# Rows of the small expert blocks scattered from a tile of their own, and weights loaded in other pieces, in an attention kernel with a routed expert layer

## The chip, the cores and the metric

One core of one Trainium2 chip runs the kernel. The metric is the device time of one execution in microseconds (us), the median over several runs. TensorE (PE in the rows, its weight loads PEld) multiplies matrices, VectorE (DVE), ScalarE (ACT) and GpSimd (POOL) work on elements, and SyncE (SP) issues most transfers (DMAs). A name with a q (ACTq, SPq) is an engine's own issuing part: it takes the instructions in order, and waits there for what an instruction needs.

## The reference, cut to what matters

```
scores = scale * (q @ k^T) - log(S);  x = sigmoid(scores) @ v     # 8 x 12 heads x 448 x 64
x = rows of 768 values, 3584 tokens
out = x                                                            # for tokens with x @ w_skip <= 0
e = argmax(x @ w_gate);  g = softmax(x @ w_gate)[e]                # 8 experts
out = x + g * (relu(x @ w1[e]) @ w2[e])                            # w1: 768 x 1024, w2: 1024 x 768
```

## The kernel before, in words

**Attention and routing.** The first 320 us or so are the attention, written out for 48 pairs of heads. Each batch's rows go to `out` as they are finished, the tokens are sorted by expert into a list in DRAM, and a small table is worked out on the chip: which blocks of tokens run, of which expert and of which kind. The first two blocks of the largest expert are written out by hand, beside the end of the attention.

**The loop over blocks.** The rest is a loop over the blocks of that table (L1535 to L1539). Each engine reads the kind of its block from the table and branches to one of four arms. A full block (`block(i, False)`) computes 128 tokens in split precision: every weight is held as a high part and a rest (`wh1`, `wl1`, `wh2`, `wl2`), and TensorE multiplies three times. A split block (`block(i, True)`) does the same, and beside it turns the raw weights of the next expert into those four sets: ScalarE writes the high parts (`hi1`, `hi2`), VectorE the rests (`lo1`, `lo2`). A half block (`half`, up to 64 tokens) and a few block (`few`, up to 32) multiply the raw weights once, in plain float32, and then load the raw weights of the next expert into the same tiles, by SyncE's queue. The order of the instructions on each engine is that of the program text; nothing is reordered by the framework.

The blocks of this input follow each other like this: split, half, full, half, full, few, full, few, full, few, split, few, full, few. The loop ends with a few block.

**What a block does with rows.** Rows come and go by indirect DMAs of GpSimd. In the block before its use, TensorE transposes the rows `xn` (`turn_x`, L489); as soon as that is done, `fetch` lets GpSimd gather the rows of the block after next into `xn` (L1269 to L1273, the gather is L561). So a gather has about one block of time. `fetch` also reads `rn` (L1270), the record that holds the rows' numbers, and ScalarE's queue loads the next record into `rn` in `next_rec` (L1105), which has to wait until L1270 has read the old one. At its end each block calls `put`: GpSimd writes the row numbers into `rp` (L1283, L1284), reads two of the results with a small add (`seen`, L1289) so that the scatter needs no wait of its own, and scatters the rows with an add into `out` (L571). L1283 overwrites what the last scatter read, so it waits until that scatter has landed.

**The rows of the results.** In a full block VectorE writes the results to `yt` and GpSimd copies them to `ys`, from which the scatter takes them. In half and split blocks VectorE writes `ys` itself. In few blocks ScalarE (L1441) and VectorE (L1443) write `yt`, and GpSimd copies it to `ys` in two halves (L1298), with a `seen` before each and one behind.

**The split block's order on ScalarE.** `whole_x`, `next_rec`, `hi2(0)`, `hi2(1)`, `hi_x`, `hi2(2)` to `hi2(5)`. On VectorE behind it: `lo2(0)` to `lo2(2)`, two casts (L1370), `lo_x` (L499), the weighted sum into `ys` (L1321), then `put` for GpSimd and `lo2(3)` to `lo2(7)`. `lo_x` reads the PSUM tile that the next block's `turn_x` writes, and the weighted sum reads the PSUM tile that the next block's second product writes.

**Raw weights.** `raw1` is held in three tiles and three loads (first half of the columns: rows 0 to 2 and 3 to 5 of the six 128-row pieces; second half: all six), `raw2` in four tiles of two pieces. Before the loop the last of the `raw2` loads goes through ScalarE's queue, the others through SyncE's.

Of the kernel before, what the change touches and what calls it, by code (L numbers as in the profile page):

```python
# [10 lines left out]
F32 = mybir.dt.float32  # L11
# [3 lines left out]
AF = mybir.ActivationFunctionType  # L15
ALU = mybir.AluOpType
# [3 lines left out]
P = 128  # L20
# [3 lines left out]
def kernel(  # L24
# [33 lines left out]
    SM = 32  # L58
# [1082 lines left out]

    parts1 = ((0, 0, 3), (0, 3, NK1), (1, 0, NK1))
    raw1g = []
    raw2g = []

    def some1(n):
        for _ in range(n):
            h, a, z = parts1[len(raw1g)]  # L1150
            raw1g.append(mo.tile([P, z - a, H1], F32, name=f"raw1_{h}_{a}"))

    def some2(n):
        for _ in range(n):
            raw2g.append(mo.tile([P, 2, DM], F32, name=f"raw2_{len(raw2g)}"))

    skips = []

    def skip(n):
        mo.tile([P, n], F32, name=f"skip_{len(skips)}")  # L1160
        skips.append(n)
# [12 lines left out]
    sv = mo.tile([P, 2, 2], F32, name="sv")  # L1174
    jk = mo.tile([P, 2], F32, name="jk")
    yt = mo.tile([P, DM], F32, name="yt")
    skip(4688 - DM)
    some1(1)
    some2(2)
    skip(128)  # L1180
    some2(2)
    raw1 = [[raw1g[i // 3][:, i % 3, :], raw1g[2][:, i, :]] for i in range(NK1)]
    raw2 = [raw2g[j // 2][:, j % 2, :] for j in range(NK2)]

    ph = [new_t(f"ph{h}") for h in range(2)]
    py = [new_t("py0"), ps_b.tile([P, 512], F32, tag="b", name="py1")]
# [3 lines left out]
    def next_expert(col):  # L1190
        return entry(NXT, col, SP, NE - 1), entry(HAS, col, SP, 1)

    def load_w1(n, nx):
        h, a, z = parts1[n]
        return nc.sync.dma_start(
            raw1g[n],
            w1[ds(nx[0], 1), a * P : z * P, h * H1 : (h + 1) * H1].rearrange(
                "o (i p) f -> p (o i) f", p=P
            ),
            cond=nx[1],  # L1200
        )

    def load_w2(g, nx, queue=nc.sync):
        queue.dma_start(
            raw2g[g],
            w2[ds(nx[0], 1), g * 2 * P : (g + 1) * 2 * P, :].rearrange(
                "o (i p) f -> p (o i) f", p=P
            ),
            cond=nx[1],
        )  # L1210
# [38 lines left out]
        nc.values_load(first_i[0:1, 0:1], engines=[ET.Activation], min_val=0, max_val=1),  # L1249
    )  # L1250

    for n in range(3):
        load = load_w1(n, nx)
        if n == 1:
            tc.add_manual_dep(
                load.ins,
                done.ins.name,
                mybir.DependencyInfo(mybir.DependencyClass.Sync, mybir.DependencyReason.DATA),
                reason="rows and code first",
            )  # L1260
        if n == 0:
            look_ahead(slice(2, 3))
    for g in range(4):
        load_w2(g, nx if g < 3 else nx_act, nc.sync if g < 3 else nc.scalar)

    def fetch():

# [10 lines left out]
    def next_rec(i):  # L1278
        load_rec(rn, ds(i + 5, 1), [ET.Activation], nc.scalar)

    def put(n, last=None):

        pool.tensor_tensor(rp[0], rid[:, 0:1], zero, op=ALU.add)  # L1283
        pool.tensor_tensor(rs, rp[0], zero, op=ALU.add)  # L1284
        if last is False:
            pool.drain()

        def seen(y, at):
            pool.tensor_tensor(  # L1289
                jk[:n], y[:n, at - 1 : at + 1], y[:n, at - 1 : at + 1], op=ALU.add  # L1290
            )

        if n == SM:

            for o in range(2):
                seen(yt, (o + 1) * H2 - 1)
                s = slice(o * H2, (o + 1) * H2)
                pool.tensor_copy(ys[:n, s], yt[:n, s])  # L1298
        if last is False:
            seen(yt, H2)  # L1300
            pool.tensor_copy(ys, yt)
        seen(ys, H2)
        out_rows = scatter(rp[0][:n], ys[:n], ALU.add)
        tc.declare_no_dep(out_rows.ins, group="got", across_iterations=True, reason="a token is in one block only")
        tc.add_to_no_dep_group("put", out_rows.ins)

    def advance(pieces=2):

# [73 lines left out]
    def few(i):  # L1382

        nx = named()
        take_rec()

        def quarter(dst, g, n, a, w, j, most):
            nc.tensor.matmul(  # L1388
                dst[g * SM : (g + 1) * SM, :n],
                a,  # L1390
                w,
                start=(j == 0),
                stop=(j == most - 1),
                tile_position=(0, g * SM),
            )

        turned = (pht[0], ph[0])
        parts = [slice(c * P, (c + 1) * P) for c in range(2)]
        for c, s in enumerate(parts):
            for j in range(NK1):  # L1400
                for g in range(4):
                    quarter(
                        ph[c], g, P, xf[:, j, :SM], raw1[j][c][:, g * P : (g + 1) * P], j, NK1
                    )
            nc.scalar.activation(hs[:, s], ph[c][:, :P], AF.Relu)
        for n in range(3):
            load_w1(n, nx)
        nc.tensor.transpose(turned[0][:, :P], hs[:, parts[0]], ident)
        for h in range(2):
            turn_x(xn, h, pxt[h])  # L1410
        fetch()
        nc.tensor.transpose(turned[1][:, :P], hs[:, parts[1]], ident)
        ht4 = ht[:, : 8 * SM].rearrange("p (c g t) -> p c g t", c=2, g=4)
        for s, p in zip(parts, turned):
            nc.scalar.activation(ht[:, s], p[:, :P], AF.Copy)
        ready_x()

        for n in range(4):
            c, j = n // 2, n % 2
            for g in range(4):  # L1420
                o, h = g // 2, g % 2
                m = 4 * c + 2 * h + j
                quarter(
                    py[h],
                    g,
                    H2,
                    ht4[:, c, 2 * h + j, :],
                    raw2[m][:, o * H2 : (o + 1) * H2],
                    n,
                    NK2 // 2,  # L1430
                )
        for g in range(4):
            load_w2(g, nx)
        look_ahead(ds(i + 3, 1))
        for m in range(2):
            for o in range(2):
                g = 2 * o + m
                s = slice(o * H2, (o + 1) * H2)
                p = py[m][g * SM : (g + 1) * SM, :H2]
                if not m:  # L1440
                    nc.scalar.activation(yt[:SM, s], p, AF.Copy, scale=recs[:SM, 0, 0:1])  # L1441
                    continue
                nc.vector.scalar_tensor_tensor(  # L1443
                    yt[:SM, s], p, recs[:SM, 0, 0:1], yt[:SM, s], op0=ALU.mult, op1=ALU.add
                )
        next_rec(i)
        put(SM)
        advance()

    def half(i):  # L1450

        nx = named()
        take_rec()

        def side(dst, g, n, a, w, j, most):
            nc.tensor.matmul(  # L1456
                dst[g * MD : (g + 1) * MD, :n],
                a,
                w,
                start=(j == 0),  # L1460
                stop=(j == most - 1),
                tile_position=(0, g * MD),
            )

        for j in range(NK1):
            for h in range(2):
                side(ph[0], h, H1, xf[:, j, :], raw1[j][h], j, NK1)
        turned = (pht[0], ph[1])
        parts = [slice(0, 2 * P), slice(2 * P, 4 * P)]
        for s in (slice(0, P), slice(P, 2 * P), parts[1]):  # L1470
            nc.scalar.activation(hs[:, s], ph[0][:, s], AF.Relu)
        for n in range(3):
            load_w1(n, nx)
# [27 lines left out]
        for g in range(4):  # L1501
# [66 lines left out]
```

## Time and profile before

| | us |
|---|---|
| median of 3 runs | 522.71 |
| lowest and highest run | 522.39, 524.77 |
| the profiled execution's own time | 522.76 |
| its span, first to last instruction | 520.4 |
| time of that execution outside its span | 2.36 |

The span is what the rows of the profile add up to; an edit that shortens the span by some amount shortens the time by the same, as the 2.36 us around it are not the kernel's instructions. In rows of the timeline the first number is the start in the span, the second the time from the first start to the last end of the instructions that are merged in that row, and the bracket tells how long the engine was idle before it and what ended that.

### The profile page before, as it was taken

How to read it: one execution, taken by the hardware profiler on the slowest of the kernel's cores; microseconds unless marked ns; L12 is line 12 of the kernel's file. 1: busy time of each engine (PE TensorE's matmuls, PEld its weight loads, DVE VectorE, ACT ScalarE, POOL GpSimd, SP SyncE). 2: the span in 40 equal slices, each digit the busy share in tenths (PEclk: the TensorE clock that was granted, in tenths of full speed). 3: DMA queues.
4: the chain of work that ended last, by engine and by line, in shares of the span. 5: the costliest groups of instructions: out<-in, count | busy, mean ns of one | idle time of the engine just before them, and what ended most of it. 6: DMA issues, size and time to landing. Idle time of an engine off the chain costs nothing.

```text
span 520.4 us, 15378 instructions
## 1 busy us (share of the span) xinstructions
PE 505.8 (97%) x5031; PEld 337.7 (65%) x5032; DVE 293.0 (56%) x692; ACT 278.3 (53%) x481; POOL 238.7 (46%) x355
## 2 busy tenths in 40 slices
PE   8999999999999999999999999999999999999991
PEld 6655545545545555555455889967769797979790
DVE  4556856658668688686694862682222322349522
ACT  5776776767767767667666212751122323258322
POOL 4523553443556675765674402232321434344534
PEclk9999999999999999999999999999999999999997
DMA  8999877997999999999965105949295879696943
GB/s 207 219 245 191 174 172 160 173 176 174 204 186 235 227 203 212 197 205 217 191 148 117 20 31 172 388 126 384 87 350 202 267 285 300 254 331 233 356 175 47
DMA packets 142082, 107.22 MB, mean 206 GB/s; under 512 B 99164, under 2 KB 114524, under 8 KB 142033
## 3 DMA queue, kind: packets, MB, share of 16 engines
q1 hardware_dynamic: 134048, 96.90, 71.3%
q0 software_dynamic: 4032, 8.51, 6.8%
q10 hardware_dynamic: 3952, 1.16, 1.1%
q8 instruction: 30, 0.49, 0.4%
q14 instruction: 20, 0.16, 0.1%
HBM read 98.49 MB, written 17.56 MB: 223 GB/s over the span
## 4 chain that ended last, share of the span: by engine, by line
PE 92%; DVE 2%; DMA 2%; issue 1%; ACT 1%; POOL 0%; ACTq 0%; POOLq 0%; DVEq 0%
PE s L209 25%; PE pa L237 23%; PE ph L513 11%; PE py L541 10%; PE b_ph L513 3%; PE b_py L541 3%; PE ph L1388 3%; PE py L1388 2%; PE ph L1456 2%; PE py L1456 2%; PE pxt L489 2%; PE pl L277 2%; PE pht L527 1%; DMA rn<-lst 1%; PE pg L294 1%
## 5 line engine op out<-in xcount | busy, mean ns | idle before, releaser
L229 ACT ACTIVATE at<-s,bias 128x896 f32<-128x896 f32 (+1 forms) x191 | 173.5, 914 | 81.2 <-PE s L209 73.2
L209 PE MATMUL s<-x 64*64 64x448 f32 (+1 forms) x1528 | 166.0, 497 | 1.7 <-DVE x L191 0.8
L237 PE MATMUL pa<-at,v 64*64 64x448 f32 (+1 forms) x1536 | 164.1, 489 | 0.0
L173 POOL COPY kq<-kq 32x896 f32<-32x896 f32 (+1 forms) x96 | 88.1, 917 | 95.9 <-DMA kq<-in_q_dram 49.6
L209 PEld LDWEIGHTS s<-x 64*64 64x64 f32 x1528 | 79.5, 191 | 54.2 <-issue 29.6
L237 PEld LDWEIGHTS pa<-at,v 64*64 64x64 f32 x1536 | 62.0, 133 | 56.4 <-issue 49.5
L191 DVE STREAM_TRANSPOSE x<-kq 128x448 f32<-128x448 f32 x94 | 80.7, 934 | 4.4 <-POOL kq L173 4.4
L247 DVE TENSOR_TENSOR xt<-xt,pa 128x448 f32<-128x448 f32 x48 | 29.8, 620 | 52.5 <-ACT xt L668 50.3
L411 POOL DMA_INDIRECT lst<-rec,idx x32 | 31.6, 987 | 16.1 <-issue 5.2
L483 POOL TENSOR_TENSOR wl<-wr,wh 128x384 fp32r<-128x384 f32 (+1 forms) x28 | 31.2, 1123 | 12.1 <-DVE wh L482 8.2
L252 DVE STREAM_TRANSPOSE y<-xt 128x448 f32<-128x448 f32 x48 | 31.0, 645 | 8.3 <-DMA out_dram<-y 6.9
L533 DVE TENSOR_TENSOR hl<-pht,hh 128x512 fp32r<-128x512 f32 x14 | 9.7, 690 | 43.3 <-ACT hh L532 29.5
L522 ACT ACTIVATE hs<-ph 128x512 f32<-128x512 f32 x14 | 8.4, 597 | 42.3 <-PE ph L513 37.6
L571 POOL DMA_INDIRECT out_dram<-ys,rp x15 | 22.8, 1519 | 16.3 <-POOLq L1535 8.4
L541 PE MATMUL py<-wh,hh 128*128 128x384 f32 x112 | 29.8, 347 | 0.0
L541 PE MATMUL py<-wh,hl 128*128 128x384 f32 x112 | 28.8, 338 | 0.0
L541 PE MATMUL py<-wl,hh 128*128 128x384 f32 x112 | 28.7, 337 | 0.0
L499 DVE TENSOR_TENSOR xl<-pxt,xh 128x384 fp32r<-128x384 f32 x30 | 15.3, 552 | 21.7 <-ACT xf L1087 20.6
L513 PE MATMUL ph<-wl,xh 128*128 128x512 f32 x84 | 26.4, 401 | 0.0
L668 ACT ACTIVATE xt<-pa 128x448 f32<-128x448 f32 x48 | 25.7, 535 | 0.8 <-PE pa L237 0.8
L513 PE MATMUL ph<-wh,xh 128*128 128x512 f32 x84 | 25.5, 400 | 0.0
L513 PE MATMUL ph<-wh,xl 128*128 128x512 f32 x84 | 24.1, 391 | 0.0
(263 smaller groups left out, 651.5 us busy)
## 6 DMA issues: line engine op xcount, KB each, us to landing
raw<-in_moe_w_dram SPq DMA_DIRECT2D x47, 768.0 KB
v<-in_v_dram SPq DMA_DIRECT2D x48, 256.0 KB
raw<-in_moe_w_dram SPq DMA_DIRECT2D x8, 1536.0 KB
out_dram<-y SPq DMA_DIRECT2D x192, 56.0 KB
kq<-in_k_dram SPq DMA_DIRECT2D x46, 224.0 KB
kq<-in_q_dram SPq DMA_DIRECT2D x46, 224.0 KB
wr<-in_moe_w_dram SPq DMA_DIRECT2D x12, 256.0 KB
wr<-in_moe_w_dram SPq DMA_DIRECT2D x16, 192.0 KB
```

The lines of the kernel that those rows point to most:

```text
L173: nc.gpsimd.tensor_copy(a[BT:, :, :, :BT], a[:BT, :, :, BT:])
L191: nc.vector.transpose(xs[:, n].rearrange("p (r j) -> p j r", j=NJ), t.rearrange("p (j d) -> p j d", d=D)[:, :, :BT],)
L209: nc.tensor.matmul(sc[m * D : (m + 1) * D, j, : qs.stop - qs.start], xs[r, 0, first::NR7], xs[r, 1, qs], start=True, stop=True,)
L229: nc.scalar.activation(at[:, :, :n], sc[:, :, :n], AF.Sigmoid, bias=bias, scale=SCALE)
L237: nc.tensor.matmul(pa[j * D : (j + 1) * D, r, qs], vt[rs, j, r + c if c < 3 else 3 * (1 - r), :], at[rs, j, : qs.stop - qs.start], start=( ...
L247: nc.vector.tensor_tensor(x, x, pa[:, 1, :S], op=ALU.add)
L252: nc.vector.transpose(y, xts[b][:, hp, :])
L411: put = nc.gpsimd.indirect_dma_start(out=lst[:, :], out_offset=bass.IndirectOffsetOnAxis(ap=idx[:, c : c + 1], axis=0), in_=rec[:, c, :], ...
L483: nc.gpsimd.tensor_tensor(lo, r, hi, op=ALU.subtract)
L513: nc.tensor.matmul(ph[h], a[:, j * P : (j + 1) * P], w[j][h], start=(n == 0), stop=(n == len(t) - 1),)
L541: last = nc.tensor.matmul(half_y(py, o), a[h][:, js], w[j][:, o * H2 : (o + 1) * H2], start=(j == 0 and n == 0), stop=(j == NK2 - 1 and n ...
L1388: nc.tensor.matmul(dst[g * SM : (g + 1) * SM, :n], a, w, start=(j == 0), stop=(j == most - 1), tile_position=(0, g * SM),)
```

## The change

Few blocks get a tile `yf` for their results. ScalarE and VectorE write `yf` in place of `yt`, and the scatter reads `yf`; the two copies to `ys` and two of the three `seen` are gone. Behind the scatter GpSimd copies two elements into `yf`, across the middle of the row. The framework makes that copy wait for the scatter that reads `yf`, and the next few block's writers of `yf` wait for the copy; the direct dependency between them and the scatter is declared away. `raw1` is now four tiles and loads of three pieces each, `raw2` three tiles and loads of two, two and four pieces; the last goes through ScalarE's queue before the loop. The tiles lie in the same places in SBUF.

```diff
-    parts1 = ((0, 0, 3), (0, 3, NK1), (1, 0, NK1))
+    w1s = iter([(h, g) for h in range(2) for g in range(2)])
...
+            raw1g[h, g] = mo.tile([P, 3, H1], F32, name=f"raw1_{h}_{g}")
...
     yt = mo.tile([P, DM], F32, name="yt")
-    skip(4688 - DM)
-    some1(1)
-    some2(2)
+    yf = mo.tile([P, DM], F32, name="yf")
+    skip(4688 - 2 * DM)
+    some1(2)
+    some2(2, 2)
     skip(128)
-    some2(2)
+    some2(4)
...
-    for g in range(4):
-        load_w2(g, nx if g < 3 else nx_act, nc.sync if g < 3 else nc.scalar)
+    for g in range(3):
+        load_w2(g, nx if g < 2 else nx_act, nc.sync if g < 2 else nc.scalar)
...
+    def freed(write):
+        tc.declare_no_dep(
+            write.ins,
+            group="sent",
+            across_iterations=True,
+            reason="GpSimd writes into both halves of the rows behind each scatter of them",
+        )
...
-        if n == SM:
-            for o in range(2):
-                seen(yt, (o + 1) * H2 - 1)
-                s = slice(o * H2, (o + 1) * H2)
-                pool.tensor_copy(ys[:n, s], yt[:n, s])
+        rows = yf if n == SM else ys
         if last is False:
             seen(yt, H2)
             pool.tensor_copy(ys, yt)
-        seen(ys, H2)
-        out_rows = scatter(rp[0][:n], ys[:n], ALU.add)
+        seen(rows, H2)
+        out_rows = scatter(rp[0][:n], rows[:n], ALU.add)
...
+        if n == SM:
+            tc.add_to_no_dep_group("sent", out_rows.ins)
+            pool.tensor_copy(yf[:n, H2 - 1 : H2 + 1], jk[:n])
...
-        for n in range(3):
-            load_w1(n, nx)
+        for h in range(2):
+            for g in range(2):
+                load_w1(g, h, nx)
...
-        for g in range(4):
+        for g in range(3):
             load_w2(g, nx)
...
-                    nc.scalar.activation(yt[:SM, s], p, AF.Copy, scale=recs[:SM, 0, 0:1])
+                    freed(nc.scalar.activation(yf[:SM, s], p, AF.Copy, scale=recs[:SM, 0, 0:1]))
...
-                    yt[:SM, s], p, recs[:SM, 0, 0:1], yt[:SM, s], op0=ALU.mult, op1=ALU.add
+                    freed(
+                        nc.vector.scalar_tensor_tensor(
+                            yf[:SM, s], p, recs[:SM, 0, 0:1], yf[:SM, s], op0=ALU.mult, op1=ALU.add
+                        )
                 )
```

## Rows read from the trace of the kernel before

**Rows 1.** The page: the span and the shares of the chain of work that ended last; then, from the waits between 341 and 503 us, the one wait of TensorE's matmuls (us in total, times, longest).
```profile
span 520.4 us, 15378 instructions
...
PE 92%; DVE 2%; DMA 2%; issue 1%; ACT 1%; POOL 0%; ACTq 0%; POOLq 0%; DVEq 0%
...
PE ph L1456 <- DMA rn<-lst: 0.3, 1, 0.3
```
**Rows 2.** The span by stretches: length, busy us of PE, PEld, DVE, ACT, POOL (instructions), granted clock of TensorE, DMA share, GB/s. The stretch from 453 holds a few block and the second split block.
```profile
453.00:478.00 25.00, 25.00 (x236) 21.25 (x234) 16.56 (x36) 17.08 (x40) 13.37 (x24) 1.00 0.84 290
478.00:503.00 25.00, 25.00 (x236) 21.24 (x234) 12.47 (x29) 8.34 (x28) 10.39 (x22) 1.00 0.83 280
```
**Rows 3.** The timeline of the last few block behind TensorE's last product, VectorE and GpSimd.
```profile
507.00 2.84 PE L1388 MATMUL py<-raw,ht 128*32 128x384 f32 x32
...
510.63 1.26 DVE L1443 SCALAR_TENSOR_TENSOR yt<-py,recs,yt 32x384 f32<-32x384 f32 x2 [0.61 <-ACT yt L1441]
511.80 0.18 POOL L1283 TENSOR_TENSOR rp<-rid,zero 128x1 int32<-128x1 int32 x1 [0.97 <-DMA out_dram<-ys,rp]
...
514.32 1.38 POOL L571 DMA_INDIRECT out_dram<-ys,rp  x1 [0.61 <-issue]
```
**Rows 4.** The timeline of GpSimd: `put` of the first few block, `fetch` of the full block behind it, and the start of that block's `put`.
```profile
415.15 0.18 POOL L1283 TENSOR_TENSOR rp<-rid,zero 128x1 int32<-128x1 int32 x1 [4.30 <-DMA out_dram<-ys,rp]
...
415.55 0.18 POOL L1289 TENSOR_TENSOR jk<-yt 32x2 f32<-32x2 f32 x1
...
416.86 0.18 POOL L1289 TENSOR_TENSOR jk<-ys 32x2 f32<-32x2 f32 x1
417.66 1.40 POOL L571 DMA_INDIRECT out_dram<-ys,rp  x1 [0.61 <-issue]
419.03 0.25 POOL L1269 TENSOR_TENSOR xn<-xn,zf 128x1 f32<-128x1 f32 x1
...
420.66 1.06 POOL L561 DMA_INDIRECT xn<-out_dram,rp  x1 [0.73 <-PE pht L527]
423.73 0.18 POOL L1283 TENSOR_TENSOR rp<-rid,zero 128x1 int32<-128x1 int32 x1 [2.01 <-DMA out_dram<-ys,rp]
```
**Rows 5.** The same of the third few block and the split block behind it.
```profile
466.80 0.65 POOL L1289 TENSOR_TENSOR jk<-yt 32x2 f32<-32x2 f32 x1
...
469.38 1.65 POOL L571 DMA_INDIRECT out_dram<-ys,rp  x1 [0.16 <-issue]
471.14 0.48 POOL L1269 TENSOR_TENSOR xn<-xn,zf 128x1 f32<-128x1 f32 x1
471.57 0.66 POOL L1270 CAST ri<-rn 128x1 int32<-128x1 f32 x1
...
475.74 0.63 POOL L1283 TENSOR_TENSOR rp<-rid,zero 128x1 int32<-128x1 int32 x1 [0.82 <-DMA out_dram<-ys,rp]
```
**Rows 6.** The timeline of all engines over the end of that split block and the start of the few block behind it.
```profile
472.62 0.34 ACTq L1105 DMA_DIRECT2D rn<-lst  x1
...
473.53 1.58 ACT L1219 ACTIVATE wh<-raw 128x768 fp32r<-128x768 f32 x2
...
475.74 3.07 ACT L1219 ACTIVATE wh<-raw 128x768 fp32r<-128x768 f32 x4
476.70 0.96 DVE L1224 TENSOR_TENSOR wl<-raw,wh 128x768 fp32r<-128x768 f32 x1 [0.38 <-issue]
...
478.29 0.56 DVE L1370 CAST wh<-raw 128x768 fp32r<-128x768 f32 x1 [0.16 <-PE py L541]
478.76 1.01 DVE L499 TENSOR_TENSOR xl<-pxt,xh 128x384 fp32r<-128x384 f32 x2
...
479.70 1.13 DVE L1321 TENSOR_SCALAR ys<-py,recs 128x384 f32<-128x384 f32 x2
...
482.05 2.84 PE L1388 MATMUL py<-raw,ht 128*32 128x384 f32 x32
```
**Rows 7.** The waits between 341 and 521 us: VectorE's idle time before the first instruction of a block, with nothing to wait for (total, times, longest).
```profile
DVE recs L1317 <- issue: 9.5, 5, 2.0
```
**Rows 8.** The gathers into `xn`: least, median and longest time to landing; and the transposes of `xn` in the second and in the last few block, with the start of the fourth few block's `put`.
```profile
DMA to landing us min/median/max: 3.7/5.9/6.6
...
431.14 0.82 PE L489 MATMUL pxt<-ident,xn 128*128 128x128 f32 x6
...
491.13 0.18 POOL L1283 TENSOR_TENSOR rp<-rid,zero 128x1 int32<-128x1 int32 x1 [3.56 <-DMA out_dram<-ys,rp]
...
506.14 0.82 PE L489 MATMUL pxt<-ident,xn 128*128 128x128 f32 x6
```
**Rows 9.** Columns as in rows 2: one us behind the end of the weights' transfers in the full block behind the first few block.
```profile
426.00:427.00 1.00, 1.00 (x8) 1.00 (x7) 0.00 (x0) 0.00 (x0) 0.00 (x0) 1.00 0.03 2
```
**Rows 10.** The timeline: weight loads of a few block on SyncE's queue; ScalarE's one wait for raw weights, in the first split block; the end of that block and the second product of the half block behind it.
```profile
404.42 2.33 SPq L1195 DMA_DIRECT2D raw<-in_moe_w_dram  x3
408.80 4.07 SPq L1204 DMA_DIRECT2D raw<-in_moe_w_dram  x4
...
333.80 0.63 ACT L1213 ACTIVATE wh<-raw 128x512 fp32r<-128x512 f32 x1 [0.85 <-DMA raw<-in_moe_w_dram]
...
343.75 1.13 DVE L1321 TENSOR_SCALAR ys<-py,recs 128x384 f32<-128x384 f32 x2
...
348.85 1.51 PE L1456 MATMUL py<-raw,ht 128*64 128x384 f32 x8
```

More of the change, by code (lines that the diff above doesn't have):

```diff
@@ L1140 @@
     mo = ctx.enter_context(tc.tile_pool(name="mo", bufs=1, reuse_waits="tile"))
-    parts1 = ((0, 0, 3), (0, 3, NK1), (1, 0, NK1))
-    raw1g = []
+    w1s = iter([(h, g) for h in range(2) for g in range(2)])
+    raw1g = {}
     raw2g = []
@@ L1149, in some1, with some2 @@
         for _ in range(n):
[L1150 to L1155, printed above, removed]
+            h, g = next(w1s)
+            raw1g[h, g] = mo.tile([P, 3, H1], F32, name=f"raw1_{h}_{g}")
+    def some2(*sizes):
+        for n in sizes:
+            raw2g.append(mo.tile([P, n, DM], F32, name=f"raw2_{len(raw2g)}"))
     skips = []
@@ L1176 @@
     yt = mo.tile([P, DM], F32, name="yt")
-    skip(4688 - DM)
-    some1(1)
-    some2(2)
+    yf = mo.tile([P, DM], F32, name="yf")
+    skip(4688 - 2 * DM)
+    some1(2)
+    some2(2, 2)
     skip(128)
-    some2(2)
-    raw1 = [[raw1g[i // 3][:, i % 3, :], raw1g[2][:, i, :]] for i in range(NK1)]
-    raw2 = [raw2g[j // 2][:, j % 2, :] for j in range(NK2)]
+    some2(4)
+    raw1 = [[raw1g[h, i // 3][:, i % 3, :] for h in range(2)] for i in range(NK1)]
+    first2 = (0, 2, 4)
+    raw2 = [raw2g[min(j // 2, 2)][:, j - first2[min(j // 2, 2)], :] for j in range(NK2)]
     ph = [new_t(f"ph{h}") for h in range(2)]
@@ L1191, in next_expert, with load_w1 @@
         return entry(NXT, col, SP, NE - 1), entry(HAS, col, SP, 1)
-    def load_w1(n, nx):
-        h, a, z = parts1[n]
+    def load_w1(g, h, nx):
         return nc.sync.dma_start(
-            raw1g[n],
-            w1[ds(nx[0], 1), a * P : z * P, h * H1 : (h + 1) * H1].rearrange(
+            raw1g[h, g],
+            w1[ds(nx[0], 1), g * 3 * P : (g + 1) * 3 * P, h * H1 : (h + 1) * H1].rearrange(
                 "o (i p) f -> p (o i) f", p=P
@@ L1205, in load_w2 @@
             raw2g[g],
-            w2[ds(nx[0], 1), g * 2 * P : (g + 1) * 2 * P, :].rearrange(
+            w2[ds(nx[0], 1), first2[g] * P : (first2 + (NK2,))[g + 1] * P, :].rearrange(
                 "o (i p) f -> p (o i) f", p=P
@@ L1250 @@
     )
-    for n in range(3):
-        load = load_w1(n, nx)
+    for n in range(4):
+        load = load_w1(n % 2, n // 2, nx)
         if n == 1:
@@ L1405, in few @@
             nc.scalar.activation(hs[:, s], ph[c][:, :P], AF.Relu)
-        for n in range(3):
-            load_w1(n, nx)
+        for h in range(2):
+            for g in range(2):
+                load_w1(g, h, nx)
         nc.tensor.transpose(turned[0][:, :P], hs[:, parts[0]], ident)
@@ L1440, in few @@
                 if not m:
-                    nc.scalar.activation(yt[:SM, s], p, AF.Copy, scale=recs[:SM, 0, 0:1])
+                    freed(nc.scalar.activation(yf[:SM, s], p, AF.Copy, scale=recs[:SM, 0, 0:1]))
                     continue
-                nc.vector.scalar_tensor_tensor(
-                    yt[:SM, s], p, recs[:SM, 0, 0:1], yt[:SM, s], op0=ALU.mult, op1=ALU.add
+                freed(
+                    nc.vector.scalar_tensor_tensor(
+                        yf[:SM, s], p, recs[:SM, 0, 0:1], yf[:SM, s], op0=ALU.mult, op1=ALU.add
+                    )
                 )
@@ L1471, in half @@
             nc.scalar.activation(hs[:, s], ph[0][:, s], AF.Relu)
-        for n in range(3):
-            load_w1(n, nx)
+        for h in range(2):
+            for g in range(2):
+                load_w1(g, h, nx)
         for h in range(2):
@@ L1500, in half @@
                 )
-        for g in range(4):
+        for g in range(3):
             load_w2(g, nx)
```

## The prediction
> **What bounds the kernel now.** First the page and the waits. The chain of work that ended last is TensorE for 92%, and between 341 and 503 us the matmuls waited once, for 0.3 us [rows 1]. The stretches say the same: in the 25 us of a few and a full or split block TensorE is busy for 25.00, at a granted clock of 1.00, which is 2.4 GHz [rows 2]. So inside the loop there is nothing to win from another engine; an edit can only put holes into TensorE's work. Then the end: TensorE's last product ends at 507.00 + 2.84 = 509.84, and 10.6 us follow without it [rows 3]. Only there can a shorter GpSimd program gain. Last, the timeline of GpSimd, block by block: how late may it be before TensorE or another engine waits for it?
>
> **What is removed.** In a few block the scatter starts 2.51 us behind L1283 (417.66 - 415.15). The new program has L1283, L1284, one `seen`, scatter. The first `seen` starts 0.40 behind L1283, and a scatter starts 0.80 behind the last `seen` (417.66 - 416.86) [rows 4], so it starts 1.20 behind L1283, 1.31 earlier.
>
> In the loop this hides behind TensorE. At the end it counts: there L1283 starts at 511.80, held by the full block's scatter, and VectorE's results are done at 510.63 + 1.26 = 511.89, before the `seen` at 512.20 [rows 3]. The last scatter moves from 514.32 to 513.00. The new small copy waits for its landing and is then in the way of the loop's end: nothing if it runs beside SyncE's own wait for that landing, about 0.5 us, near the 0.61 of issuing before the last scatter [rows 3], if GpSimd's closing instructions follow it. I take 0.2. **End: -1.1 us, -1.3 to -0.8.**
>
> **What is added: a wait on GpSimd's queue.** The two-element copy (bounded by the 0.18 us of a `seen` [rows 4]) costs nothing itself. It waits for the scatter. A few block's scatter delayed the next writer of what it reads, L1283, to 6.07 us behind its start (423.73 - 417.66) [rows 4], and 6.36 before the split block [rows 5]. Until now that wait stood behind `fetch`, where it held up nothing; now it stands before it. Queued behind the copy are the loop's turn to the next block, `fetch` (L1269 to the gather) and the next `put`. For the turn, the rows bound: 1.37 us from a scatter to L1269 (419.03 - 417.66) [rows 4], 1.76 in the split block (471.14 - 469.38) [rows 5], and 1.9 of idle time on VectorE before a block's first instruction (9.5/5) [rows 7]. I take 1.7, and 1.9 in the split block.
>
> The Trainium skill (DMA: Bandwidth & Descriptors, "Rules for kernel authors") advises to issue a DMA early and to wait on its semaphore late; this edit waits at once. By its formula ("Anatomy of one DMA") of 2.0 us plus bytes over 436e3, 32 rows of 3 KB would be an estimated 2.2 us; the trace's 6.07 decides here. By 2.2 the time would be that of the first rival below, 521.6.
>
> *Full block behind a few block.* With L1283 at t: scatter t+1.2, copy t+7.3, L1269 t+9.0, gather 1.63 later (420.66 - 419.03) [rows 4], t+10.6. For the first few block that is 425.8 instead of 420.66. The rows are needed at 431.14 [rows 8]. Gathers landed in 3.7 to 5.9 (median) to 6.6 us. The weights' transfers have ended by 426 [rows 9]; a gather that starts at their end should be near the short end, so 4.2: lands 430.0, 1.1 us to spare. The fourth few block: t = 491.13, gather 501.7, lands 505.9, needed at 506.14 [rows 8], 0.2 to spare. No stall, but thin; at the median of 5.9 each would be late, by 0.6 and 1.5. `next_rec` there waits for L1270 too, but ScalarE has nothing behind it until the next block.
>
> *Split block behind the third few block.* Here ScalarE has work behind `next_rec`. The `seen` at 466.80 stays, so the scatter moves from 469.38 to 467.6; the copy starts 6.36 later at 474.0, L1269 at 475.9. L1270 ends 0.4 (two instructions of 0.18) to 1.1 us later (471.57 + 0.66 - 471.14) [rows 5]; VectorE is waiting then, so I take the short one: 476.3, before 472.23. ScalarE's load of `rn` followed that end by 0.39 (472.62), `hi2(0)` the load by 0.91 (473.53) [rows 6]: 477.6 instead of 473.53, 4.1 late. Late next are, in order: `hi2(2)`, which starts 2.21 behind `hi2(0)` (475.74 - 473.53) and takes some 0.85, ends 480.7; `lo2(2)`, 0.96, 481.8; two casts, 0.56 each less 0.1, 482.8; `lo_x`, 1.01 less 0.1 (478.29 + 0.56 - 478.76), 483.7; the weighted sum, 1.13 less 0.1, 484.75. TensorE's second product of the few block cannot overwrite that PSUM before; it started at 482.05 [rows 6]. Stall 2.7, and once, as what is late on VectorE afterwards (`lo2(3)` to `lo2(7)`) is needed only in the full block. The gather there starts at 475.9 + 1.6 = 477.5, lands at 482, within the same hole. With L1270 at its slow end the stall is 3.5; with a turn of 1.4 it is 2.2. **Split block: +2.7 us, +2.2 to +3.5.**
>
> **Loads.** Seven issues per block before and after; one more for `raw1` and one less for `raw2` shift SyncE's queue by one issue of about 0.8 (2.33 us for three) [rows 10], with over 20 us until the weights are used. Waiting on smaller `raw1` tiles could take ScalarE's 0.85 us in the first split block away; waiting for four pieces of `raw2` together could delay its `hi2(4)` and casts, by at most the time of two pieces, 786 KB at 345 GB/s (290 at a share of 0.84 [rows 2]), 2.3 us. Both hide behind TensorE: the weighted sum at the end of that block is done at 344.88, its PSUM is wanted at 348.85 [rows 10], 4 us of cover. If that cover were used up, each us beyond would count. In the second split block `hi2(4)` is late by more than any wait for the weights. I take 0, bounds -0.3 (the one wait of the matmuls [rows 1], if it goes) to +0.9 (a wait like ScalarE's 0.85, if TensorE felt it).
>
> **Sum.** 522.76 (the profiled execution: span 520.4 and 2.36 around it) - 1.1 + 2.7 + 0 = 524.4; the profiled one is 0.05 over the median of 522.71, so 524.3.
>
> **The rivals.** A change of 0.5% of 522.71, 2.6 us, is about what a measurement tells from none; "same" is 520.1 to 525.3.
> - *The hold is short or absent:* the scatter lands soon, or GpSimd runs into the next block while the copy waits, so L1270 ends before about 473.5, which ScalarE hardly feels. For it: most of those 6 us were no idle time, as the gather stood between. Against: L1283 was still waiting then [rows 4, 5]. Time 522.71 - 1.1 = 521.6. The skill's 2.2 us estimate above leads here; the rows speak against it.
> - *Late rows, slower:* the gathers moved in three full blocks land at the median 5.9 or later, and `turn_x` of the few blocks (L489) waits. It decides from a landing of about 5.4 us for the second few block (431.14 - 425.8), 4.4 for the last (506.14 - 501.7). For it: 5.9 is the median [rows 8]. Against: that median holds gathers that ran beside weights [rows 2, 9]. At 5.9 the second few block loses 0.6, the third about as much, the last 1.5: 2.7 on top of the forecast, 527.0.
> - *Split block worse than its sum:* with 3.5 us there and 0.8 at the end, 525.4; with one late gather 526.
> - *Gain over 0.5%:* nothing in the rows gives it, as TensorE has no hole in the loop.
>
> **How the numbers follow.** Forecast (522.7 to 525.3) 0.49, short hold (521.2 to 522.7) 0.21, late rows or a worse split block (over 525.3) 0.26, faster by over 0.5% 0.04. Faster 0.04, same 0.70, slower 0.26. The range takes in the short hold and the late rows: 521.2 to 527.0; the forecast's own is 523.3 (522.71 - 1.3 - 0.3 + 2.2) to 525.3.
>
> **What would show it.** Right: a few block's scatter about 1.2 us behind L1283; L1269 of the next block some 9 us behind L1283 instead of 3.9; in the second split block the load of `rn` near 476.7 and `hi2` right behind it; a hole in TensorE before L1388's second product of the fourth few block; the end 9.5 us behind TensorE's last product. Wrong: L1269 soon behind the scatter; no hole there; or holes before L489 in other few blocks, with `xn` as what ended them.

## The result: 5 us slower, all of it behind the second split block

| | before | after |
|---|---|---|
| median of 6 runs each, same chip | 524.14 us (522.39 to 525.40) | 528.60 us (527.23 to 529.91) |
| ratio, 95% interval | | 1.0095 (1.0080 to 1.0111) |
| profiled execution (span) | 522.76 (520.4) | 528.69 (525.9) |

The forecast was 524.3 us with a range of 521.2 to 527.0. The change costs about 5 us. The forecast was counted from the 522.71 of the first three runs of before; against the 524.14 of all six the change adds 4.5 us, by the ratio 5.0, where +1.6 was forecast.

Of the waits of TensorE's matmuls in the whole span, the three that lie in the loop:

```profile
PE ph L1396 <- ACT xh L495: 1.4, 1, 1.4
...
PE ph L1396 <- ACT wh L1220: 0.7, 2, 0.4
PE ph L1421 <- ACT hs L1413: 0.7, 1, 0.7
```

Line numbers have moved: L1388 is now L1396 (both products of a few block), L1283 L1293, L1269 L1270, L1219 L1220, L1408 and L1412 L1417 and L1421, L1321 L1329; the small copy is L1313. The second stretch of [rows 2] (in the first TensorE is busy for 25.00 us as before), then the place of the loss (busy us of PE, PEld, DVE, ACT, POOL; clock; DMA share; GB/s):

```profile
478.00:503.00 25.00, 22.15 (x204) 16.86 (x204) 13.96 (x30) 11.37 (x27) 9.43 (x16) 0.93 0.83 276
478.00:482.00 4.00, 2.17 (x30) 1.26 (x29) 2.51 (x3) 3.78 (x7) 2.26 (x4) 1.00 0.34 97
482.00:485.00 3.00, 2.66 (x44) 1.86 (x48) 3.00 (x7) 1.76 (x4) 0.00 (x0) 0.50 0.47 143
485.00:488.00 3.00, 2.33 (x44) 1.84 (x36) 2.96 (x6) 0.45 (x2) 2.02 (x3) 0.93 0.95 322
```

TensorE, busy throughout before, now has holes from 478 on, and behind the first of them runs at a granted clock of 0.50 (1.2 GHz) for some 3 us. That is the fourth few block, behind the second split block. Here is that place, all engines in order of time; it answers to [rows 5, 6].

```profile
475.20 0.54 POOL L1313 COPY yf<-jk 32x2 f32<-32x2 f32 x1 [4.66 <-DMA out_dram<-yf,rp]
477.16 0.19 POOL L1270 TENSOR_TENSOR xn<-xn,zf 128x1 f32<-128x1 f32 x1 [1.42 <-PE py L541]
477.77 0.34 ACTq L1105 DMA_DIRECT2D rn<-lst  x1
478.22 1.58 ACT L1220 ACTIVATE wh<-raw 128x768 fp32r<-128x768 f32 x2 [3.81 <-POOL rq L1273]
478.51 0.52 PE L541 MATMUL py<-wh,hl 128*128 128x384 f32 x2
480.42 0.71 PE L1396 MATMUL ph<-raw,xf 128*32 128x128 f32 x16 [1.39 <-ACT xh L495]
480.44 3.04 ACT L1220 ACTIVATE wh<-raw 128x768 fp32r<-128x768 f32 x4
...
482.27 3.95 PE L1396 MATMUL ph<-raw,xf 128*32 128x128 f32 x72 [0.41 <-ACT wh L1220]
483.60 2.35 PEld L1396 LDWEIGHTS ph<-raw,xf 128*32 128x32 f32 x56 [0.50 <-issue]
484.12 1.13 DVE L1329 TENSOR_SCALAR ys<-py,recs 128x384 f32<-128x384 f32 x2
...
487.48 0.28 ACT L1413 ACTIVATE hs<-ph 128x128 f32<-128x128 f32 x1 [2.72 <-PE pxt L489]
487.81 0.33 PE L1421 MATMUL ph<-ident,hs 128*128 128x128 f32 x1 [0.67 <-ACT hs L1413]
488.13 3.00 PE L1396 MATMUL py<-raw,ht 128*32 128x384 f32 x32
491.06 1.21 PE L513 MATMUL ph<-wh,xh 128*128 128x512 f32 x4
```

And the same of TensorE before:

```profile
477.74 0.51 PE L541 MATMUL py<-wh,hl 128*128 128x384 f32 x2
478.18 2.83 PE L1388 MATMUL ph<-raw,xf 128*32 128x128 f32 x96
...
484.81 1.66 PE L513 MATMUL ph<-wh,xh 128*128 128x512 f32 x6
```

I measure each kernel by the same stretch: from TensorE's last pair of L541 in the split block to the first L513 of the full block behind the few block. Before it is 484.81 - 477.74 = 7.07 us, after 491.06 - 478.51 = 12.55: **5.48 lost**. The hold is read against the same pair: `hi2` starts 4.21 ahead of it before (473.53 in [rows 6]) and 0.29 ahead of it after, 3.9 late.

The rows split the 5.48. The weight load at 483.60 is the one behind ScalarE's last conversion (480.44 + 3.04 = 483.48); 56 of the first product's 96 matmuls are left there. It stands 5.1 behind the pair; before, with all 96 in 2.83 us, that point lay an estimated 1.6 behind it (478.18 + 40/96 of 2.83 - 477.74). So 3.5 of the loss is the wait for the held conversions. The 56 matmuls then take 2.62 in place of an estimated 1.65, 1.0 more, at the lower clock. From their end to the second product it is 1.9 in place of 1.0, as the second half's relu (`hs`) starts late; no run shows why. The last 0.2 is the second product itself.

The span grew by 5.5. The pair is 0.77 later than before already (478.51 - 477.74), which the change did not make: the second few block's `turn_x` is at 431.90 in place of 431.14 [rows 8], with no hole in TensorE since the loop began, and TensorE's first L513 behind the attention, 284.66 before and 285.87 after, lies at 283.61 to 287.02 in the runs below, which do the same up to there. The end gave back as much: 0.77 + 5.48 - 0.77 = 5.5.

The timeline of the end, TensorE's last product and GpSimd behind it, answering to [rows 3]:

```profile
513.27 2.84 PE L1396 MATMUL py<-raw,ht 128*32 128x384 f32 x32
518.40 0.20 POOL L1293 TENSOR_TENSOR rp<-rid,zero 128x1 int32<-128x1 int32 x1 [1.25 <-DVE sv L1319]
519.58 1.36 POOL L571 DMA_INDIRECT out_dram<-yf,rp  x1 [0.58 <-POOL jk L1299]
523.03 0.18 POOL L1313 COPY yf<-jk 32x2 f32<-32x2 f32 x1 [2.09 <-DMA out_dram<-yf,rp]
```

and the two scatters in the chain of work that ended last (start, length):

```profile
512.56 5.70 DMA out_dram<-ys,rp
...
519.58 3.29 DMA out_dram<-yf,rp
```

From the product's end (516.11) to the end of the span it is 9.8 us, before 10.56.

### The profile page after: what moved, and what is told of

It is laid out like the page before. It is cut to its first block, busy times and chain, and to the rows that moved or that the text cites. A ratio compares the mean times of both kernels' runs of the same rounds, so it can differ in the third digit from the quotient of the medians.

```text
span 525.9 us, 15388 instructions
## 1 busy us (share of the span) xinstructions
PE 509.6 (97%) x5031; PEld 340.9 (65%) x5032; DVE 294.6 (56%) x692; ACT 278.1 (53%) x481; POOL 230.4 (44%) x340
## 4 chain that ended last, share of the span: by engine, by line
PE 89%; DVE 4%; DMA 3%; ACT 1%; issue 1%; POOL 1%; SPq 0%; ACTq 0%; POOLq 0%; DVEq 0%
PE s L209 23%; PE pa L237 21%; PE ph L513 11%; PE py L541 11%; PE b_ph L513 3%; PE b_py L541 3%; PE ph L1396 3%; PE py L1396 2%; PE py L1467 2%; PE ph L1467 2%; PE pxt L489 2%; PE pl L277 1%; PE pht L527 1%; DMA out_dram<-ys,rp 1%; PE pg L294 1%
## 5 line engine op out<-in xcount | busy, mean ns | idle before, releaser
L541 PE MATMUL py<-wh,hh 128*128 128x384 f32 x112 | 29.8, 347 | 0.0
L541 PE MATMUL py<-wh,hl 128*128 128x384 f32 x112 | 28.8, 338 | 0.0
L541 PE MATMUL py<-wl,hh 128*128 128x384 f32 x112 | 28.7, 337 | 0.0
L513 PE MATMUL ph<-wl,xh 128*128 128x512 f32 x84 | 26.3, 400 | 0.0
L513 PE MATMUL ph<-wh,xh 128*128 128x512 f32 x84 | 25.5, 400 | 0.0
L513 PE MATMUL ph<-wh,xl 128*128 128x512 f32 x84 | 24.1, 391 | 0.0
L571 POOL DMA_INDIRECT out_dram<-ys,rp x10 | 15.6, 1561 | 13.7 <-POOLq L1547 8.4
```

Source lines behind the costliest of these rows:

```text
L513: nc.tensor.matmul(ph[h], a[:, j * P : (j + 1) * P], w[j][h], start=(n == 0), stop=(n == len(t) - 1),)
L541: last = nc.tensor.matmul(half_y(py, o), a[h][:, js], w[j][:, o * H2 : (o + 1) * H2], start=(j == 0 and n == 0), stop=(j == NK2 - 1 and n ...
```

## The experiments

The theory after seeing the result, A: the small copy waits for the scatter on GpSimd, so `next_rec` and ScalarE's `hi2` in the second split block are held, and TensorE with them. Its rivals: the new loads (L), late rows (R, G). "Lost" is always the stretch above against 7.07. Ratios are to runs of the kernel before on the same chip.

| kernel | ratio (95%) | `hi2` late | lost |
|---|---|---|---|
| changed kernel | 1.0095 (1.0080 to 1.0111) | 3.9 | 5.48 |
| loads alone | 0.9986 (0.9970 to 1.0002) | 0.0 | 0.00 |
| hold alone | 1.0176 (1.0151 to 1.0201) | 5.3 | 6.95 |
| copy moved | 0.9969 (0.9954 to 0.9983) | 0.0 | 0.00 |
| copy moved, old loads | 0.9968 (0.9949 to 0.9986) | 0.0 | 0.00 |
| record last | 1.0073 (1.0047 to 1.0100) | 0.0 | 1.91 |
| activations at the blocks' ends | 1.0177 (1.0146 to 1.0208) | 1.0 | 3.07 |
| activations behind `xf` | 1.0090 (1.0068 to 1.0112) | 4.0 | 5.34 |
| the same and VectorE's behind `lo_x` | 1.0068 (1.0045 to 1.0091) | 4.1 | 5.02 |
| the same and 11 idle matmuls | 1.0114 (1.0071 to 1.0157) | 4.1 | 3.82 |
| changed kernel and 20 idle matmuls | 1.0278 (1.0243 to 1.0313) | 3.4 | 4.42 |
| changed kernel and 15 idle matmuls | 1.0189 (1.0155 to 1.0224) | 3.4 | 3.35 |

**The loads alone.** The new groups of loads, with `yt`, the copies and `ys` of before.

> The kernel before with the new grouping of the weight loads alone (four and three); the small blocks' rows keep yt, the two copies by GpSimd and ys. Theory A (GpSimd's new copy behind the scatter holds ScalarE in the second split block, and TensorE with it): the time of before within 0.9 us (at most 0.2%), TensorE goes on between the second split block and the fourth small one without a hole, clock at 2.4 GHz there. Rival L (the loads make the loss: other conversions become late, or the first product of the small block does): about 5 us (1.0%) slower than before, with the hole of 1.4 to 1.9 us ahead of the fourth small block's first product still there.

No wait of TensorE from 341 us on, nothing lost; rival L falls. Whether the loads win 0.1% stays open, as the interval touches 1.

**The hold alone.** Into the kernel before:

```diff
         tc.add_to_no_dep_group("put", out_rows.ins)
+        if n == SM:
+            pool.tensor_tensor(ys[:n, H2 - 1 : H2 + 1], jk[:n], jk[:n], op=ALU.add)
```

> The kernel before, with its loads and its copies, and one more GpSimd instruction behind each small block's scatter, a two-element addition that writes into the two middle columns of ys, so that it waits for the scatter as the new copy does. Nothing at the end is shortened. Theory A: ScalarE's L1220-like conversions of the second split block are held about 4 us by the load of the next record, TensorE has a hole ahead of the fourth small block's first product, the clock falls to 1.2 GHz there for some 3 us, and the kernel is 5 to 6.5 us (1.0 to 1.2%) slower than before. What the record's two-element addition costs at the very end is nothing more than 0 to 3 us, since it runs behind the last scatter, on which the end waits anyway. Rival L (loads): within 0.9 us of before.

One GpSimd instruction of 0.2 us, 9 us (1.76%) slower: the sign is theory A's, the size more than expected. TensorE's waits in the loop:

```profile
PE ph L1390 <- ACT xh L495: 2.8, 1, 2.8
PE ph L1390 <- DMA rn<-lst: 1.4, 1, 1.4
```

Here the copies stand ahead of the scatter, so the hold is 1.4 longer. The wait of 1.4 is a second way in which it reaches TensorE: the third few block's first product waits until the held load of `rn` has landed, which it doesn't read.

**The copy moved** to the next larger block's `put`:

```diff
+        if n != SM:
+            pool.tensor_copy(yf[:SM, H2 - 1 : H2 + 1], jk[:SM])
         out_rows = scatter(rp[0][:n], rows[:n], ALU.add)
@@
-            pool.tensor_copy(yf[:n, H2 - 1 : H2 + 1], jk[:n])
```

> The changed kernel with the two-element copy moved: not behind the small block's scatter but ahead of the scatter of the next larger block, where the small block's scatter has long landed. Theory A: nothing on GpSimd waits behind a small block's scatter, ScalarE's conversions in the second split block start within 0.5 us of where they do in the kernel before, no hole, no clock drop, and what is left is the shorter end: 0.7 to 1.3 us faster than before, 5.2 to 6.5 us faster than the changed kernel. Rival L: about 5 us slower than before still. Rival R (rows gathered late because GpSimd's scatter and gather follow more closely): between the two, with waits of turn_x for the gather.

The same stretch, 478 to 503:

```profile
478.00:503.00 25.00, 25.00 (x238) 21.25 (x242) 12.71 (x29) 8.05 (x27) 9.73 (x19) 1.00 0.81 280
```

and the end, last product and last scatter:

```profile
506.69 2.84 PE L1397 MATMUL py<-raw,ht 128*32 128x384 f32 x32
...
513.13 1.36 POOL L571 DMA_INDIRECT out_dram<-yf,rp  x1 [0.57 <-issue]
```

TensorE is busy for 25.00 of 25.00 us there again at full clock, and the time is 0.31% (1.6 us) under before's: the wait behind the scatter is the whole of the loss, and the kernel without it beats both. Its end is 519.1 - 509.53 = 9.6 us behind the last product, 1.0 less than before.

**The copy moved, with before's loads.**

> The kernel before with its own loads, the small blocks' rows in yf with no copy by GpSimd, and the two-element copy ahead of the next larger block's scatter, as in the run that moved it. Theory A: no hole; the end is 0.8 to 1.2 us shorter and nothing else changes: ratio 0.9977 to 0.9985. If the new loads give the 0.7 us (0.14%) that they alone showed, this is that much slower than the run with both (0.9969); if that was chance, as fast.

0.9968, as fast as with the new loads. The gain lies in the rows' own tile; the end is 519.3 - 510.00 = 9.3 us here.

**The record last.** The changed kernel, in split blocks only:

```diff
-        next_rec(i)
+        if not last:
+            next_rec(i)
@@
             for j in range(2, NK2 - 2):
                 hi2(j)
+            next_rec(i)
```

> The changed kernel with one line moved in the split blocks alone: the load of the next record is issued by ScalarE behind all its conversions there, no longer ahead of hi2. GpSimd's copy still waits for the scatter, its additions still end as late. Theory A: the wait is still in ScalarE's queue, but nothing of the split block is behind it; TensorE has no hole ahead of the fourth small block, no clock drop, and the time is 0.3 to 1.3 us under before's. Rival L (loads): stays 5 us slower than before. Rival G (GpSimd's lateness itself costs, by the gather and the rows of the next blocks, not by ScalarE's queue): 3 to 5 us slower than before, with waits of TensorE for xn.

A miss by half: `hi2` is on time, and the profiled run loses 1.91 in the stretch in place of 5.48, but the median is 0.73% over before's. (The profiled one, at 524.59, is the fastest of six, the slowest 529.16; so the trace explains only part of the median's loss.) TensorE's waits in the loop:

```profile
PE ph L1468 <- DMA rn<-lst: 1.1, 1, 1.1
PE ph L1397 <- DMA rn<-lst: 0.7, 1, 0.7
PE pxt L489 <- DMA xn<-out_dram,rp: 0.5, 1, 0.5
```

The landing of the record holds the next block's first product, behind the first split block too, and a gather comes late (rival G, 0.5 us). Out of ScalarE's way, the late record still finds TensorE.

**Why does the first product wait at all?** It reads `xf`, which ScalarE had finished before the hold, and not `hi2`. Theory C: a block waits for work of the block before by the count of an engine's instructions; the kinds of block differ, and the count is right for all of them only from the end of a block backwards. In split blocks six conversions (`hi_x` twice, then `hi2(2)` to `hi2(5)`) stand last on ScalarE, where full and half blocks have the six `xf` copies. So I put work that nothing reads behind the copies in the other blocks:

```diff
+    def behind():
+        for j in range(8):
+            nc.scalar.activation(tk[:, j : j + 1], zf, AF.Copy)
```

First at the ends of full, half and few blocks.

> The changed kernel with eight one-element-a-row activations into a tile of their own at the end of ScalarE's work in the full, half and small blocks, not in the split ones. Nothing reads them. Theory C (the first product of a block waits for xf by ScalarE's instruction count, counted back from the end of the block before, so in the split block its six waits fall on the last six ScalarE instructions, the held conversions, not on the xf copies): with eight more behind xf elsewhere the same waits fall on instructions ahead of the held hi2. The fourth small block's first product then starts as soon as the record in rn has landed, near 479.2 on the changed kernel's clock, and runs through. Its relu must still queue behind ScalarE's last conversion (483.49), so the second product starts near 485.6 in place of 488.13 and the loss from the split block to the full one behind it is 2.8 to 3.3 us in place of 5.5: 2 to 3 us faster than the changed kernel, 1 to 3 us slower than before (ratio near 1.004). Rival D (the first product truly needs those conversions, or waits for something else): hole and loss as in the changed kernel, ratio near 1.0095.

The expected ratio was missed, and that is the plainest evidence for C. TensorE's waits in the loop:

```profile
PE ph L513 <- ACT tk L1331: 8.9, 4, 2.2
```

Four times the block behind a few block waits 2.2 us for `tk`, which nothing reads. The fourth few block's first product runs without a hole (484.99, 2.83 us). As TensorE had lost 2.2 us by then, the hold was short there, so this run gives no size. Then behind `xf` itself:

> As the run with eight activations at the blocks' ends, but they stand directly behind the xf copies in the full, half and small blocks, so that in small blocks they run before the weighted rows and no next block waits for them. TensorE then keeps its distance to GpSimd, and the hold in the second split block is as long as in the changed kernel (hi2 near 478.2 on its clock). Theory C (counts): the fourth small block's first product starts within 0.5 us of the end of the split block's last product and runs without a hole; its relu queues behind the held conversions (483.5), the second product starts some 2.5 us earlier than in the changed kernel; from the split block to the full block behind the small one 2.8 to 3.5 us are lost in place of 5.5, ratio 1.004 to 1.006. Rival D (first product needs the conversions): 5.5 lost, ratio 1.0095.

The fourth few block, TensorE:

```profile
481.04 2.83 PE L1399 MATMUL ph<-raw,xf 128*32 128x128 f32 x96 [0.39 <-DMA rn<-lst]
...
486.55 0.30 PE L1420 MATMUL pht<-ident,hs 128*128 128x128 f32 x1 [2.68 <-DVE ys L1332]
...
487.25 0.85 PE L489 MATMUL pxt<-ident,xn 128*128 128x128 f32 x6 [0.41 <-DVE recs L1324]
488.14 4.48 PE L1399 MATMUL py<-raw,ht 128*32 128x384 f32 x32
```

and the stretch of its second product:

```profile
488.00:491.50 3.50, 3.50 (x26) 1.38 (x28) 3.50 (x6) 2.51 (x17) 3.35 (x4) 0.52 1.05 402
```

The first product starts as the record lands and runs through, as C says. Yet 5.34 are lost: the hole has moved. The transposes wait for VectorE's weighted sum and then for `recs`, none of which they touch, and the clock, 0.52, now falls on the second product, which takes 4.48 in place of 2.84 us. Next the same eight dummies on VectorE, behind `lo_x`:

> As the run with eight activations behind the xf copies, with eight one-element-a-row copies by VectorE behind lo_x in the same three kinds of block too. In that run the fourth small block's first transposes waited for VectorE's weighted sum and its copies of recs in the split block, none of which they read or overwrite. Theory C for VectorE (those waits are counts from the end of the block too): they fall on earlier instructions now, the first transpose follows the relu (485.05 there), and only the second product waits for the weighted sum, whose PSUM it overwrites; it starts at the end of the sum, some 1.2 us earlier than in that run, which is the forecast's own chain: 2.4 to 2.7 us late, plus up to 1.7 if the clock still falls. Loss over the stretch 2.4 to 4.2 in place of 5.3; ratio 1.004 to 1.007. Rival (the transposes truly need the sum or the copies): loss 5.3, ratio 1.009.

The same place:

```profile
484.01 1.13 DVE L1334 TENSOR_SCALAR ys<-py,recs 128x384 f32<-128x384 f32 x2
484.34 0.85 PE L489 MATMUL pxt<-ident,xn 128*128 128x128 f32 x6 [0.41 <-DVE xl L499]
485.68 4.70 PE L1401 MATMUL py<-raw,ht 128*32 128x384 f32 x32 [0.39 <-ACT ht L1429]
```

The waits for the sum and for `recs` are gone. What is left on TensorE's path is a true one: `turn_x` overwrites `pxt`, which `lo_x` reads. The second product starts 3.15 late (7.46 us behind the pair at 478.22; before 482.05 - 477.74 = 4.31), in the run before this one 3.69 late. It then takes 4.70 in place of 2.84, at a clock of 0.52 from 486 to 489, though not all of the 1.86 is the clock's, as the last run shows. Loss 5.02, over what I expected.

**The clock.** The changed kernel with idle matmuls of `ident` by `ident` behind each split block's last product, first 20:

```diff
+        if last:
+            for _ in range(20):
+                nc.tensor.matmul(pht[0][:, :P], ident, ident, start=True, stop=True)
         advance(1 if last else 2)
```

> The changed kernel with 20 matmuls of ident by ident (128 columns, into a tile that is free) behind the last product of each split block, so that TensorE is busy while the fourth small block's first product waits. They cost some 4.2 us at the first split block, where nothing waits; only the stretch from the second split block to the full block behind the fourth small one is read. Theory K (1.9 us of the 5.5 lost there is the clock, which fell to 1.2 GHz after the hole): clock at 2.4 GHz through the stretch, first product from 483.4 to about 486.1 counted from the changed kernel's start of the split block, the full block some 1.0 to 1.9 us earlier in the stretch, loss 3.6 to 4.5 in place of 5.5. Rival (the clock fell for another reason, or the late start alone makes the loss): the stretch loses 5.5 as before, or the clock falls all the same. The whole is 2 to 3.5 us slower than the changed kernel.

The clock stays at 1.00 through the stretch and 4.42 are lost, but the matmuls (4.63 us) outlast the wait and set that figure themselves. By the ratios the whole is 9.6 us slower than the changed kernel, not 2 to 3.5; 3.7 of it is a hole behind the first split block (last section). So 15:

> As the run with 20 idle matmuls behind each split block's last product, with 15 (3.5 us), so that they end before ScalarE's last conversion and don't set the end of the wait themselves. Theory K (about 2 us of the 5.5 is the clock): clock at 2.4 GHz, first product ends some 2 us earlier against ScalarE's last conversion than in the changed kernel (1.7 to 2.1 us behind it, there 3.9), 3.4 to 4.0 us lost in that stretch in place of 5.5. Rival (lateness alone): 4.6 to 5.5 lost. If the hole of 3.7 us that the 20 matmuls had ahead of the first half block is there again, it is no matter of their number; with it the whole is 5 to 7 us slower than the changed kernel, without it 1 to 3.

The stretches behind these matmuls:

```profile
482.00:485.00 3.00, 3.00 (x29) 3.00 (x28) 2.67 (x4) 3.00 (x7) 1.31 (x3) 1.00 0.46 131
485.00:488.00 3.00, 3.00 (x99) 2.48 (x97) 2.96 (x9) 1.09 (x3) 0.19 (x1) 1.00 0.11 5
```

Clock 1.00, TensorE busy throughout, 3.35 lost in place of 5.48. The hold was 0.5 shorter in this run, but that is no part of the gain, as these matmuls too set the start of the first product, which waits for nothing behind them:

```profile
485.16 2.92 PE L1399 MATMUL ph<-raw,xf 128*32 128x128 f32 x96
```

Its last 56 matmuls begin an estimated 5.0 us behind the pair (485.16 + 40/96 of 2.92 - 481.37), in the changed kernel 5.1. From there on the changed kernel loses 2.0 us more: the 1.0 of the slower matmuls, the 0.9 ahead of the second product and the 0.2 in it, none of which is seen here. That the 0.9 comes from the clock is not shown. Where the hole had moved, the clock alone cost 1.64 (4.48 against 2.84) on the second product. The whole missed its range: by the ratios 4.9 us slower than the changed kernel in place of 1 to 3, the profiled executions 1.6 apart.

**All together:** dummies on both engines and 11 idle matmuls.

> The run before this one with 11 idle matmuls (2.5 us) behind each split block's last product, so that TensorE has no long hole. If hold, counts and clock are the whole of the loss, what is left in the stretch is the forecast's term alone, 2.5 to 2.8 us from the split block to the full block behind the small one, at 2.4 GHz throughout. The idle matmuls cost 2.5 us more at the first split block, so the whole is no faster than the run before this one. If something else costs there, 3.5 or more is left.

The clock stays at 1.00 and the second product starts 3.14 late, as without the idle matmuls. But 3.82 are lost, not 2.5 to 2.8: the second product takes 3.50 us at full clock, 0.66 more than before. The rows show where:

```profile
487.38 4.43 DVE L1230 TENSOR_TENSOR wl<-raw,wh 128x768 fp32r<-128x768 f32 x5
487.71 3.50 PE L1404 MATMUL py<-raw,ht 128*32 128x384 f32 x32 [0.39 <-ACT ht L1432]
488.41 0.19 PEld L1404 LDWEIGHTS py<-raw,ht 128*32 128x32 f32 x8 [0.58 <-issue]
```

After two weight loads TensorE pauses until 488.41. The first of the five instructions of VectorE, `lo2(3)`, ends 0.07 ahead of that (487.38 + 0.96 for one, as in [rows 6]); in the run before this one the pause ends at 486.38, again 0.07 behind the end of `lo2(3)` (485.35 + 0.96). Theory C fits: TensorE goes on there to the half of `py` that VectorE reads in few blocks, fifth from the end of its work, and fifth from the end in a split block stands `lo2(3)`. No run tests this. With it the second product's clock cost in the run before this one is 1.2 (4.70 against 3.50).

## Why the prediction was wrong, step by step

- **Scatter, copy and the lateness of `fetch`: right.** Behind the first few block, answering to [rows 4]:

```profile
416.68 0.18 POOL L1293 TENSOR_TENSOR rp<-rid,zero 128x1 int32<-128x1 int32 x1 [5.03 <-DMA out_dram<-ys,rp]
417.84 1.38 POOL L571 DMA_INDIRECT out_dram<-yf,rp  x1 [0.58 <-POOL jk L1299]
423.82 0.18 POOL L1313 COPY yf<-jk 32x2 f32<-32x2 f32 x1 [4.60 <-DMA out_dram<-yf,rp]
425.37 0.19 POOL L1270 TENSOR_TENSOR xn<-xn,zf 128x1 f32<-128x1 f32 x1 [1.37 <-PE py L541]
```

  The scatter stands 1.16 behind L1293 (forecast 1.2), the copy 6.0 behind the scatter (6.07), the next block's first instruction 8.7 behind L1293 (9.0). The rule that the Trainium skill gives (DMA: Bandwidth & Descriptors, "Rules for kernel authors"), to issue early and wait late, is borne out by the two positions of one copy: 5.48 us lost behind the scatter, 0.00 a block later.
- **Late rows: did not come.** With 0.2 to 1.1 us to spare by the forecast, no transposition of `xn` waits for a gather in the changed kernel.
- **ScalarE's hold: right.** 4.1 forecast, 3.9 measured. The chain through `lo2(2)`, casts, `lo_x` and weighted sum too: the sum ends at 485.25, 6.74 behind the pair, and the second product started 4.31 behind it before. Had it waited for the sum alone it would be 2.43 late, where the forecast had 2.7.
- **"TensorE's second product cannot overwrite that PSUM before": the step that failed, +2.7 where 5.48 was measured.** True, but other waits come first. The first product, which the forecast let run, cost 3.5 by itself, and what followed it 2.0. In order of what the runs showed: (1) the few block's transposes ahead of the second product overwrite `pxt` and so wait for `lo_x`, which the section on the kernel before names and the forecast's chain passes over; with the work between them the second product is 3.15 late, 0.5 over the forecast, and inside it a pause of 0.7 follows, by its timing for `lo2(3)`. So at full clock 3.82 are lost. (2) By VectorE's count they wait longer, 3.69. (3) The first product waits by ScalarE's count for the held conversions. Before, the same waits were there, and the conversions ended in time. (4) Behind the holes the clock falls to 1.2 GHz: 1.0 us on the first product in the changed kernel, 1.6 and 1.2 on the second in the two runs where the hole had moved. These don't add up one by one: taking (3) away alone gained 0.14, taking (2) and (3) 0.46, as the hole and with it the slow clock only moved; keeping TensorE busy alone gained 2.1.
- **The end: right in kind, a little short of its range.** -0.77 measured, -1.1 forecast (-1.3 to -0.8). L1293 came 0.3 later behind the last product than before (2.29 us; 511.80 - 509.84 in [rows 3]), as the full block's scatter took 5.70 to land (512.56 + 5.70 = 518.26; the row names VectorE, which was done about then too); the trailing copy made the scatter's way to the end 6.32 in place of 6.08, 0.24 where I had 0.2. Without the copy there the gain was 1.0 and 1.3.
- **The loads: right,** 0 within the measurement.

The range failed for one reason: its upper end priced later gathers and a longer hold, but none of its cases let a hole change the speed of what came behind it, or let TensorE wait for an instruction that it has no use for. The forecast's own upper bound, 525.3, is also less than its terms give (522.71 - 0.8 + 0.9 + 3.5 = 526.3), but 527.0 covers that.

## What to carry to other kernels

A wait put at the end of one block's queue is paid where the next block is tightest: look for the DMA or register that another engine's queue takes from this one, and then for everything behind it. Where different blocks run in one loop, read a wait as "so many instructions of that engine must be done", not as the data that it stands for: work at the end of a block holds the next block, used or not, and what follows a hole in a saturated TensorE may run at the lower clock as well. A guard that must wait for a scatter belongs where the scatter has long landed: that made this change a gain of 0.3%.

## What the runs showed of the hardware

- The clock does not answer to the length of a hole alone. In the run with the activations at the blocks' ends TensorE had the same hole of 2.2 us, ahead of the same product, four times; it ran at 1.2 GHz for part of the 4 us behind the first and at 2.4 GHz behind the other three. TensorE had been busy at 1.00 in the 4 us ahead of the first two holes alike. The stretches right behind these two:

```profile
410.50:414.50 4.00, 3.98 (x11) 3.18 (x12) 0.25 (x3) 0.34 (x4) 0.18 (x1) 0.61 1.06 293
439.40:443.40 4.00, 4.00 (x18) 3.29 (x19) 0.18 (x2) 0.29 (x4) 0.13 (x1) 1.00 1.05 292
```

- The same 32-row scatter landed in 3.29 us at the end, with nothing beside it, and in 5.8 to 5.9 in the loop, where it released its next writer at 6.0 (423.82 - 417.84). By the Trainium skill (DMA: Bandwidth & Descriptors, "Anatomy of one DMA") it would be an estimated 2.2 us; the quickest scatter that the traces here show took 3.1.
- With 20 idle matmuls TensorE stood still for 3.7 us behind the first split block, before a product that waited for nothing that the profile shows; with 15 it did not. What ended it was not found.
